# A fused FFT filter and ELU feed-forward kernel: the first eleven steps regrouped in small PSUM tiles, the last step issued one step earlier

## The chip, the core and the metric

The kernel runs on one core of a Trainium2 chip. The metric is the device time of one execution in microseconds (us), lower is better. Beside it stands one profiled execution, taken by the hardware profiler, from which all durations here come.

The engines: PE (TensorE, matmuls), ACT (ScalarE), DVE (VectorE), POOL (GpSimd), SP (issues DMAs), and the DMA queues. Each engine takes its instructions in the order in which the program hands them over, and waits on semaphores of others.

## The reference: what is computed

For 8 batches of a sequence of 3008 rows by 256 columns:

```python
X = np.fft.rfft(x, axis=1)
Yr = Xr @ w_r - Xi @ w_i + b_r
Yi = Xr @ w_i + Xi @ w_r + b_i
Y = soft_threshold(Yr, 0.01) + 1j * soft_threshold(Yi, 0.01)
y = np.fft.irfft(Y, n=3008, axis=1).astype(np.float32)
h = y.reshape(8 * 3008, 256) @ moe_w_in          # 256 -> 2048
g = np.where(h > 0, h, np.exp(np.minimum(h, 0)) - 1)
out = g @ moe_w_out                              # 2048 -> 256
```

So: a Fourier transform over the sequence, a complex matrix product with bias, a soft threshold, the transform back, and a two-layer feed-forward net with an ELU between its layers.

## The kernel before, in words

**The Fourier part.** 3008 is taken as 47 times 64, and each transform is two small matrix products with a trip through DRAM between them. Per batch there are units named by their kind: A (6 of them: M1 times x, `unit_A`, matmuls at line 145), X (8: `unit_X`, line 176), M (12: the complex product, `unit_M`, line 193), B (6: `unit_B`, line 245) and Y (8: `unit_Y`, line 400, which write `yT`, the transposed input of the feed-forward net). A is stored to DRAM (`DA`), and `load_Z` brings it back in the order that X wants; B is stored to `DB`, and `load_Bs` brings it back for Y. Each unit writes one PSUM tile of two banks and copies it out, mostly on ACT (`evac`, lines 126 and 128).

**The feed-forward part.** Tokens go in blocks of 512, hidden columns in pairs of 128. One step is one pair of one block: 8 steps to a block, 47 steps to a batch (`PER`), 376 steps in all (`n`). A step's first layer, `front`, is four matmuls into the tile `hps` (line 844, halves s = 0 and 1, each a bank of 512 columns). Then the ELU: Exp on ACT from `hps` to `Et`, a clamp of `Et`, and a combination with `hps` on DVE into `gT`. There are three ways: for a step with no unit beside it, and for step 0, in halves, Exp at line 853, clamp on POOL at line 881, combination at line 869; for a step with an M unit, two ACT passes (lines 855 and 856) and line 869; otherwise Exp on the whole tile (line 858), clamp on DVE (line 883), combination at line 871. The second layer, `back`, is eight matmuls (line 902) that add into two one-bank tiles `ps_o` over the block's eight steps; after the eighth, the block is copied to `osb` (line 913) and stored (line 920).

**The order of the work is written out by hand** in the last loop. Step i issues: the units that `plan` puts in `f0`, then `front(i)`, then the `gT` of step i-1 (`finish_elu`), then what `plan` puts in `f1`, then the clamp of step i (`elu`), then `back(i-2)`. A Fourier unit so rides along with nearly every step, and works on the next batch.

**PSUM** has eight banks: `psF`, one tile of two banks, used by all units in turn and by `front` in every third of some free steps; `psH`, two tiles of two banks for `front`; `psO`, two banks for `back`. Before the loop, batch 0 is brought through the Fourier part alone, with pools of its own that are closed one after the other; the last of these (`lateA`, `chain`, `lateB`) hold `turn_back` (line 368), `first_Y` (line 386), half of an A unit of batch 1 (`spare_A`, line 290) and the third B unit of batch 0 (`split_B`, line 309).

**The first eleven steps** work on batch 0 while the rest of its Y units and the A units of batch 1 are still to be done. `plan(0)` puts the A units u = 1 to 5 of batch 1 in `f1` of steps 0 to 4, and the Y units u = 2 to 7 of batch 0 in `f0` of steps 5 to 10. `load_Bs` for those Y units is in `f1` of steps 1 and 3, `load_Z` for batch 1 in `f1` of step 5; a scaling of a quarter of `w_in` (line 707, DVE) is in `f1` of steps 1 to 4. The X units of batch 1 begin at step 11.

**The last step** is 375: after its `front` come `back(373)`, `back(374)` and `back(375)`; its clamp runs half on DVE and half on POOL, halves are hidden columns, and the second layer takes all of half 0 first.

Of the kernel before, what the change touches and what calls it, by code (L numbers as in the profile page):

```python
# [19 lines left out]
N1 = 47  # L20
# [9 lines left out]
def kernel(  # L30
# [96 lines left out]
        else:  # L127
            nc.scalar.copy(dst, src)  # L128

    def unit_A(b, u, alone=False, on_dve=False, ahead=False):  # L130
# [12 lines left out]
        ps = unit_ps("aps", alone or ahead)  # L143
        for j in range(2):
            nc.tensor.matmul(  # L145
                ps[:, j, :], lhsT=M1[:],
                rhs=xt[:, 4 * uu + 2 * j : 4 * uu + 2 * j + 2, :], start=True, stop=True,
            )
        evac(
            A[:, 4 * uu : 4 * uu + 4, :].rearrange("p n d -> p (n d)"),  # L150
            ps[:].rearrange("p a b -> p (a b)"), on_dve,
        )
# [210 lines left out]
    def turn_back(dt):  # L363

        for h in range(2):
            ps = one_bank()
            for j in range(4):
                nc.tensor.matmul(
                    ps[0 : 16 * NT, j * P : j * P + P],
                    lhsT=turned[0][:, dt, 4 * h + j, :], rhs=idm[:], start=True, stop=True,  # L370
                )
            evac(
                Bs_of[0, 0][0 : 16 * NT, 4 * h : 4 * h + 4, dt * P : dt * P + P],
                ps[0 : 16 * NT, :].rearrange("p (m d) -> p m d", d=P), bool(h),
            )

    def first_Y(dt):

        if dt == 0:
            yT_of[0] = late2.tile([P, 2, S], BF16, name="yT", tag="yT")  # L380
        yv = yT_of[0][:, dt, 0:WT].rearrange("p (r j) -> p r j", j=8)
        for h in range(2):
            ps = one_bank()
            pv = ps[:].rearrange("p (k j) -> p k j", j=P)[:, :, 0 : 2 * N1]
            for j in range(4):
                nc.tensor.matmul(
                    pv[:, j], lhsT=Bs_of[0, 0][:, 4 * h + j, dt * P : dt * P + P], rhs=M4[:],
                    start=True, stop=True,
                )
            evac(yv[:, :, 4 * h : 4 * h + 4], pv.rearrange("p j r -> p r j"), bool(h))  # L390
# [390 lines left out]
    for h, w in enumerate((w40, w41)):  # L781
# [3 lines left out]
    gate(Bs_of[0, 0][64:96, 0, 0:1])  # L785
    load_w_out(1)
    first.close()
    lateA, chain, lateB = (
        second.enter_context(
            tc.tile_pool(name=n_, bufs=k_, space=bass.MemoryType.PSUM, reuse_waits="tile")  # L790
        )
        for n_, k_ in (("lateA", 2), ("chain", 4), ("lateB", 2))
    )
    turn_back(0)
    turn_back(1)
    keep_A = spare_A()
    first_Y(0)
    first_Y(1)
    keep_B = split_B(2, two_banks(lateB, "lateB"), True)
    keep_A()  # L800
    keep_B()
    scale_w_in(1, True, 1)
    second.close()

    psF = ctx.enter_context(
        tc.tile_pool(name="psF", bufs=1, space=bass.MemoryType.PSUM, reuse_waits="tile")
    )
# [3 lines left out]
    psO = ctx.enter_context(  # L811
        tc.tile_pool(name="psO", bufs=2, space=bass.MemoryType.PSUM, reuse_waits="tile")
    )


    g_of = {}
# [12 lines left out]
    def front(i, third, on_act, halves):  # L829
        blk, fp = divmod(i, NPAIR)  # L830
        if third:
            hps = psF.tile([P, 2, TB], F32, name="hps", tag="fps")
        else:
            hps = psH.tile([P, 2, TB], F32, name="hps", tag="hps")
        todo = []
        for s in range(2):
            ft = 2 * fp + s
            for piece in sorted(pieces(blk * TB, TB), key=lambda z: z[3] - z[2]):
                todo.append((s, ft, piece))
        if i == PER // NPAIR * NPAIR:  # L840
            todo.sort(key=lambda z: z[2][0])
        for s, ft, (b, t0, c0, c1) in todo:
            for dt in range(2):
                nc.tensor.matmul(  # L844
                    hps[:, s, c0:c1], lhsT=w_in_s[:, dt, ft * P : ft * P + P],
                    rhs=yT_of[b][:, dt, t0 : t0 + c1 - c0],
                    start=(dt == 0), stop=(dt == 1),
                )
        Et = late3.tile([P, 2, TB], F32, name="Et", tag="Et")
        E_ = Et[:]  # L850
        if halves:
            for s in range(2):
                nc.scalar.activation(E_[:, s], hps[:, s], AF.Exp)  # L853
# [7 lines left out]
    late_elu = []  # L861

    def finish_elu():
        for i, hps, Et, whole, halves in late_elu:
            gT = late3.tile([P, 2, TB], F32R, name="gT", tag="gT")
            for s in range(2) if halves else (slice(0, 2),):
                o, h, e = gT[:, s], hps[:, s], Et[:, s]
                if whole:
                    nc.vector.scalar_tensor_tensor(o, e, -1.0, h, ALU.add, ALU.max)  # L869
                else:  # L870
                    nc.vector.scalar_tensor_tensor(o, h, 0.0, e, ALU.max, ALU.add)  # L871
            g_of[i] = gT
        late_elu.clear()

    def elu(i, hps, Et, on_pool, on_act):

        E_ = Et[:]
        if on_pool:
            for s in range(2):
                eng = nc.vector if i == n - 1 and s == 0 else nc.gpsimd  # L880
                eng.tensor_scalar(E_[:, s], E_[:, s], 1.0, 0.0, ALU.min, ALU.max)  # L881
        elif not on_act:
            nc.vector.tensor_scalar(E_, E_, 1.0, -1.0, ALU.min, ALU.add)  # L883
        late_elu.append((i, hps, Et, on_pool or on_act, on_pool))

    def back(i, split):
# [7 lines left out]
            ]  # L894
        po = po_of[blk]
        order = [(q, s) for q in range(nq) for s in range(2)]
        if i == n - 1:
# [12 lines left out]
        last = i == n - 1  # L910
        for q in range(nq):
            copy = nc.vector.tensor_copy if (last and q) or (split and q == 0) else nc.scalar.copy
            copy(osb[:, 2 * q : 2 * q + 2, :], po[q][:])  # L913
            for i_ in range(2 * q, 2 * q + 2):
                for b, t, c0, c1 in pieces(bs + i_ * P, P):
                    ov = out[b * S : b * S + S, :].rearrange("(r w j) e -> w r j e", w=4, j=8)
                    while c0 < c1:
                        w, r0 = t // WT, t % WT // 8
                        k = min(c1 - c0, (w + 1) * WT - t)
                        (nc.scalar if last and i_ % 2 == 0 else nc.sync).dma_start(  # L920
                            ov[w, r0 : r0 + k // 8], osb[c0 : c0 + k, i_, :]
                        )
                        t, c0 = t + k, c0 + k
# [5 lines left out]
    def plan(b):  # L929
# [10 lines left out]
        if n1 < B:  # L940
# [4 lines left out]
                xs = (3, 8, 13)  # L945
                seq += [("A", 5), ("n", 0), ("n", 1)]
            else:
                seq = (
                    [("a", u) for u in range(1, 6)] + [("y", u) for u in range(2, 8)]
                    + [u for u in mid if u[0] != "A"]  # L950
                    + [("A", 0), ("A", 1), ("n", 0), ("n", 1)]
                    + [("A", u) for u in range(2, 6)]
                )
                xs = (10, 13, 16)
        else:
            lead, seq = 0, [("y", u) for u in range(2, 8)]
        for t, u in enumerate(seq, lead):
            if u[0] == "y":
                f0[t].append(put("Y", b, u[1]))
            elif u[0] == "n":  # L960
                f0[t].append(put("Y", n1, u[1]))
            elif u[0] == "a":
                f1[t].append(put("A", n1, u[1]))
            elif u[0] == "A":
                if n2 < B:
                    f0[t].append(put("A", n2, u[1]))
# [8 lines left out]
        if b == 0:  # L975
            for t in range(4):
                f1[t + 1].append((scale_w_in, (2 + t // 2, True, t % 2)))
            f1[1].append((load_Bs, (0, 1)))
            f1[3] += [(load_Bs, (0, w)) for w in (2, 3)]
            f1[5] += [(load_Z, (1, s0, s1)) for s0, s1 in ((0, 8), (8, NS))]  # L980
# [5 lines left out]

    f0 = f1 = None
    bare = 0
    for i in range(n + LAG):
        if i < n:  # L990
            r = i % PER
            if r == 0:
                f0, f1 = plan(i // PER)
# [7 lines left out]
            h = front(i, calm and bare % 3 == 1, on_act, free or i == 0)  # L1001
        finish_elu()
        if i < n:
            for f, a in f1[r]:
# [1 line left out]
            split = i > LAG and (i - LAG) % NPAIR == NPAIR - 1  # L1006
            if split:
                back(i - LAG, True)
            elu(i, *h, free or i == 0, on_act)
        else:  # L1010
            split = False
        if i >= LAG and not split:
            back(i - LAG, False)


# [28 lines left out]
```

## Time and profile before

| what | value |
|---|---|
| times of the runs shown | 908.20, 910.53, 910.32 us; median 910.32 |
| the profiled execution's own time | 908.42 us |
| its span | 906.6 us |
| granted TensorE clock, mean | 0.999 |
| busy: PE / DVE / ACT / POOL | 888.8 / 719.7 / 698.5 / 312.8 us |
| HBM traffic | 116 GB/s over the span |

The span is what the profile covers, from first to last recorded work; the execution's own time is 1.8 us more. "Busy" sums the durations of an engine's instructions. The profile has these views: a timeline of instructions (start, duration, engine, line, operation, output and inputs, count), a list of waits, a table of busy time in stretches, a chain of work that ended last, and groups of instructions by line.

### The profile page before, as it was taken

What the parts mean: (1) busy time and instruction counts of PE and PEld (TensorE: products, weight loads), DVE (VectorE), ACT (ScalarE), POOL (GpSimd) and SP (SyncE); (2) the same over time, 40 slices, a digit from 0 to 9 for tenths busy, and PEclk for the clock granted to TensorE, in tenths of its full rate; (3) what the DMA queues carried; (4) which work ended last, traced back from release to release, by engine and by line L of the source; (5) the groups of instructions that cost most, each with busy time, mean ns of one, the idle gap of its engine ahead of it and who ended that gap; (6) DMA issues with size and microseconds to landing.
All of it is one profiled execution on the core that took longest, in us unless ns stands there. A gap on an engine that the chain in (4) does not pass through costs nothing.

```text
span 906.6 us, 17374 instructions
## 1 busy us (share of the span) xinstructions
PE 888.8 (98%) x6767; PEld 652.3 (72%) x6767; DVE 719.7 (79%) x899; ACT 698.5 (77%) x857; POOL 312.8 (34%) x436
## 2 busy tenths in 40 slices
PE   8889999999999999999999999999999999999997
PEld 3458667776678676876678766787667867777776
DVE  8779778887788778887788877888778877778776
ACT  6688778787878788788787888778887877777664
POOL 6710440133331431405404153133332134443664
PEclk9999999999999999999999999999999999999999
DMA  8988025821383215723176032752228111231011
GB/s 263 315 242 252 25 71 158 238 70 48 94 231 117 71 48 156 197 91 93 52 204 186 26 105 59 212 161 77 65 75 228 31 42 47 82 83 48 24 47 47
DMA packets 90655, 106.06 MB, mean 117 GB/s; under 512 B 5302, under 2 KB 81340, under 8 KB 87212
## 3 DMA queue, kind: packets, MB, share of 16 engines
q1 hardware_dynamic: 84316, 77.42, 30.9%
q0 software_dynamic: 5968, 27.26, 9.1%
q8 instruction: 53, 0.87, 0.4%
q10 hardware_dynamic: 288, 0.26, 0.1%
q14 instruction: 30, 0.25, 0.1%
HBM read 55.12 MB, written 49.81 MB: 116 GB/s over the span
## 4 chain that ended last, share of the span: by engine, by line
PE 85%; DMA 4%; DVE 4%; ACT 3%; issue 2%; POOL 1%; SPq 0%; DVEq 0%; ACTq 0%; POOLq 0%
PE ps_o L902 34%; PE hps L844 34%; PE mps L193 9%; PE yps L400 2%; PE bps L245 2%; PE aps L145 2%; PE xps L176 2%; DMA DB<-Bz 1%; DMA Z<-DA 1%; DVE gT L871 1%; DMA xt<-in_x_dram 1%; DMA Bs<-DB 1%; DVE Et L883 1%; DVE gT L869 1%; ACT Et L858 1%
## 5 line engine op out<-in xcount | busy, mean ns | idle before, releaser
L902 PE MATMUL ps_o<-w_out_r,gT 128*128 128x256 f32 x3008 | 476.6, 301 | 0.2 <-DVE gT L869 0.2
L902 PEld LDWEIGHTS ps_o<-w_out_r,gT 128*128 128x128 f32 x3008 | 403.5, 189 | 49.9 <-DVE osb L913 1.3
L844 PE MATMUL hps<-yT,w_in_s 128*128 128x512 bf16 (+4 forms) x1728 | 388.7, 352 | 1.3 <-DVE gT L871 0.3
L869 DVE SCALAR_TENSOR_TENSOR gT<-Et,hps 128x512 fp32r<-128x512 f32 (+1 forms) x268 | 220.3, 851 | 74.3 <-POOL Et L881 38.2
L871 DVE SCALAR_TENSOR_TENSOR gT<-hps,Et 128x1024 fp32r<-128x1024 f32 x200 | 244.7, 1223 | 15.8
L844 PEld LDWEIGHTS <-w_in_s 128*128 128x128 bf16 x1728 | 141.7, 98 | 128.7 <-issue 20.7
L858 ACT ACTIVATE Et<-hps 128x1024 f32<-128x1024 f32 x200 | 206.1, 1030 | 10.2 <-PE hps L844 3.5
L881 POOL TENSOR_SCALAR Et<-Et 128x512 f32<-128x512 f32 x183 | 109.1, 615 | 221.7 <-ACT Et L853 218.7
L883 DVE TENSOR_SCALAR Et<-Et 128x1024 f32<-128x1024 f32 x200 | 138.4, 692 | 47.9 <-ACT Et L858 40.2
L211 POOL TENSOR_SCALAR clip<-yb 128x512 f32<-128x512 f32 x84 | 51.6, 615 | 317.1 <-DVE yb L203 279.6
L853 ACT ACTIVATE Et<-hps 128x512 f32<-128x512 f32 x184 | 99.9, 595 | 63.7 <-PE hps L844 63.7
L855 ACT ACTIVATE Et<-hps 128x1024 f32<-128x1024 f32 x84 | 86.3, 1027 | 71.9 <-PE hps L844 71.4
L212 POOL TENSOR_TENSOR Y<-yb,clip 128x512 bf16<-128x512 f32 x84 | 107.2, 1277 | 7.0
L856 ACT ACTIVATE Et<-Et 128x1024 f32<-128x1024 f32 x84 | 88.8, 1057 | 2.7
L203 DVE TENSOR_TENSOR yb<-mps,bias_bc 128x512 f32<-128x512 f32 x89 | 61.3, 689 | 35.4 <-PE mps L193 26.8
L128 ACT CAST XT<-xps 128x768 bf16<-128x768 f32 x61 | 48.7, 800 | 17.1 <-PE xps L176 17.1
L193 PE MATMUL mps<-wcat_r,XT 128*128 128x512 bf16 x192 | 58.2, 384 | 1.0 <-ACT Bz L258 0.5
L128 ACT CAST yT<-yps 128x752 bf16<-128x752 f32 x62 | 48.9, 789 | 12.5 <-PE yps L400 12.4
L193 PE MATMUL mps<-wcat_s,XT 128*128 128x512 bf16 x192 | 57.1, 379 | 0.0
L128 ACT CAST A<-aps 128x1024 bf16<-128x1024 f32 x45 | 45.6, 1014 | 13.8 <-PE aps L145 12.0
L193 PEld LDWEIGHTS <-XT 128*128 128x128 bf16 x384 | 30.9, 98 | 29.8 <-issue 0.7
L258 ACT CAST Bz<-bps 128x1024 bf16<-128x1024 f32 x45 | 45.0, 1001 | 2.1 <-PE bps L245 2.1
(132 smaller groups left out, 415.4 us busy)
## 6 DMA issues: line engine op xcount, KB each, us to landing
xt<-in_x_dram POOLq DMA_DIRECT2D x21, 1024.0 KB, 7.3
out_dram<-osb SPq DMA_DIRECT2D x158, 128.0 KB
Bs<-DB SPq DMA_DIRECT2D x30, 384.0 KB
DA<-A SPq DMA_DIRECT2D x20, 512.0 KB
DB<-Bz SPq DMA_DIRECT2D x20, 512.0 KB
Z<-DA SPq DMA_DIRECT2D x7, 1152.0 KB
Z<-DA SPq DMA_DIRECT2D x11, 384.0 KB
xt<-in_x_dram POOLq DMA_DIRECT2D x6, 512.0 KB, 6.2
```

The lines of the kernel that those rows point to most:

```text
L128: nc.scalar.copy(dst, src)
L193: nc.tensor.matmul(ps, lhsT=XT[:, dt, c, o : o + P], rhs=wm[:, dt, :], start=(not biased and m == 0 and dt == 0), stop=(m == 1 and dt == 1),)
L212: nc.gpsimd.tensor_tensor(Y_of[b, q][:, i, :], yb, clip[:], ALU.subtract)
L844: nc.tensor.matmul(hps[:, s, c0:c1], lhsT=w_in_s[:, dt, ft * P : ft * P + P], rhs=yT_of[b][:, dt, t0 : t0 + c1 - c0], start=(dt == 0), sto ...
L853: nc.scalar.activation(E_[:, s], hps[:, s], AF.Exp)
L856: nc.scalar.activation(E_, E_, AF.Exp, scale=-1.0)
L858: nc.scalar.activation(E_, hps[:], AF.Exp)
L869: nc.vector.scalar_tensor_tensor(o, e, -1.0, h, ALU.add, ALU.max)
L871: nc.vector.scalar_tensor_tensor(o, h, 0.0, e, ALU.max, ALU.add)
L881: eng.tensor_scalar(E_[:, s], E_[:, s], 1.0, 0.0, ALU.min, ALU.max)
L883: nc.vector.tensor_scalar(E_, E_, 1.0, -1.0, ALU.min, ALU.add)
L902: nc.tensor.matmul(po[q][:, i_ % 2, :], lhsT=gT[:, s, i_ * P : i_ * P + P], rhs=w_out_r[:, ft, :], start=(ft == 0 and i_ % 2 == 0), stop=( ...
```

## The change

1. **No `psF` in the first eleven steps** (`FILL = 11`). Its two banks are two one-bank tiles of a pool `psG` until step 11. The A and Y units of these steps use one `psG` tile for each half, and each half has its own copy out (half 0 on ACT, half 1 on DVE; both on ACT for the A unit of step 1). `split_Y` is the new form of a Y unit.
2. **Units moved**: A units to steps 1, 3, 4, 5, 6; Y units to steps 7 to 10, two in steps 7 and 10; `load_Bs` to steps 2, 4, 5; `load_Z` to step 6; the next x loads on POOL from steps 10, 13, 16 to 12, 15, 18.
3. **ELU of steps 0 to 10** always in halves with the clamp on POOL, and the Exp of half 0 is handed over between the two halves of the first layer (`early`).
4. **`back(0)` goes ahead of `front(2)`**, and takes all of half 0 first.
5. **The last step**: `front(375)` is issued ahead of `back(372)`, in `psF`; its Exp, clamp and combination are split by tokens instead of hidden columns, the clamp all on POOL; its second layer is in the usual order; the second half of the last block is copied out and stored in two pieces. In the last batch the steps that use `psF` are shifted by one.
6. **Before the loop**: `turn_back` and `first_Y` swap ACT and DVE for their two copies; the copy of `split_B` goes half to ACT; the late pools change their places.

```diff
+        if apart:
+            pair = two_banks(psG, "gps")
+            banks = [t[:] for t in pair]
...
-                ps[0 : 16 * NT, :].rearrange("p (m d) -> p m d", d=P), bool(h),
+                ps[0 : 16 * NT, :].rearrange("p (m d) -> p m d", d=P), not h,
...
+    def split_Y(b, u):
+        w, dt = u // 2, u % 2
+        yv = yT_of[b][:, dt, w * WT : w * WT + WT].rearrange("p (r j) -> p r j", j=8)
+        for h, t in enumerate(two_banks(psG, "gps")):
+            pv = t[:].rearrange("p (k j) -> p k j", j=P)[:, :, 0 : 2 * N1]
+            for j in range(4):
+                nc.tensor.matmul(
+                    pv[:, j], lhsT=Bs_of[b, w][:, 4 * h + j, dt * P : dt * P + P], rhs=M4[:],
+                    start=True, stop=True,
+                )
+            evac(yv[:, :, 4 * h : 4 * h + 4], pv.rearrange("p j r -> p r j"), bool(h))
...
-    keep_B = split_B(2, two_banks(lateB, "lateB"), True)
+    keep_B = split_B(2, two_banks(lateB, "lateB"), False)
...
+        early = i < FILL
         for s, ft, (b, t0, c0, c1) in todo:
             for dt in range(2):
                 nc.tensor.matmul(
                     hps[:, s, c0:c1], lhsT=w_in_s[:, dt, ft * P : ft * P + P],
...
+            if early and (dt, c1) == (1, TB):
+                nc.scalar.activation(E_[:, s], hps[:, s], AF.Exp)
+        if early:
+            return hps, Et
+        if i == n - 1:
+            for h in range(2):
+                t = slice(TB // 2 * h, TB // 2 * h + TB // 2)
+                nc.scalar.activation(E_[:, :, t], hps[:, :, t], AF.Exp)
...
+            for t, u in ((1, 1), (3, 2), (4, 3), (5, 4), (6, 5)):
+                f1[t].append((unit_A, (1, u, False, t > 1, True)))
+            for t, a, u in ((7, f0, 2), (7, f1, 3), (8, f0, 4), (9, f0, 5), (10, f0, 6), (10, f1, 7)):
+                a[t].append((split_Y, (0, u)))
+            for t, w in ((2, 1), (4, 2), (5, 3)):
+                f1[t].append((load_Bs, (0, w)))
...
+        if i == LAG:
+            back(0, False)
...
-            elu(i, *h, free or i == 0, on_act)
+            elu(i, *h, free or i < FILL, on_act)
+            if i == n - 2:
+                early_h = front(n - 1, True, False, True)
```

More of the change, by code (lines that the diff above doesn't have):

```diff
@@ L128, in evac, with unit_A @@
             nc.scalar.copy(dst, src)
-    def unit_A(b, u, alone=False, on_dve=False, ahead=False):
+    def unit_A(b, u, alone=False, on_dve=False, apart=False):
         ci, uu = u // 2, u % 2
@@ L142, in unit_A @@
         dav = DA_of[b].rearrange("j p d -> p j d")
-        ps = unit_ps("aps", alone or ahead)
+        if apart:
+            pair = two_banks(psG, "gps")
+            banks = [t[:] for t in pair]
+        else:
+            ps = unit_ps("aps", alone)
+            banks = [ps[:, j, :] for j in range(2)]
         for j in range(2):
             nc.tensor.matmul(
-                ps[:, j, :], lhsT=M1[:],
+                banks[j], lhsT=M1[:],
                 rhs=xt[:, 4 * uu + 2 * j : 4 * uu + 2 * j + 2, :], start=True, stop=True,
             )
[L149 to L152, printed above, removed]
+        Af = A[:, 4 * uu : 4 * uu + 4, :].rearrange("p n d -> p (n d)")
+        if apart:
+            for j in range(2):
+                evac(Af[:, 512 * j : 512 * j + 512], banks[j], on_dve and bool(j))
+        else:
+            evac(Af, ps[:].rearrange("p a b -> p (a b)"), on_dve)
         j0 = 8 * ci
@@ L387, in first_Y @@
                     pv[:, j], lhsT=Bs_of[0, 0][:, 4 * h + j, dt * P : dt * P + P], rhs=M4[:],
+                    start=True, stop=True,
+                )
+            evac(yv[:, :, 4 * h : 4 * h + 4], pv.rearrange("p j r -> p r j"), not h)
+    def split_Y(b, u):
[6 more added lines that the diff above has]
+                    pv[:, j], lhsT=Bs_of[b, w][:, 4 * h + j, dt * P : dt * P + P], rhs=M4[:],
                     start=True, stop=True,
@@ L787 @@
     first.close()
-    lateA, chain, lateB = (
+    chain, lateB, lateA = (
         second.enter_context(
@@ L791 @@
         )
-        for n_, k_ in (("lateA", 2), ("chain", 4), ("lateB", 2))
+        for n_, k_ in (("chain", 4), ("lateB", 2), ("lateA", 2))
     )
@@ L803 @@
     second.close()
-    psF = ctx.enter_context(
-        tc.tile_pool(name="psF", bufs=1, space=bass.MemoryType.PSUM, reuse_waits="tile")
-    )
     psH = ctx.enter_context(
@@ L813 @@
     )
+    few = ExitStack()
+    psG = few.enter_context(
+        tc.tile_pool(name="psG", bufs=2, space=bass.MemoryType.PSUM, reuse_waits="tile")
+    )
+    FILL = 11
     g_of = {}
@@ L841, in front @@
             todo.sort(key=lambda z: z[2][0])
+        Et = late3.tile([P, 2, TB], F32, name="Et", tag="Et")
+        E_ = Et[:]
+        early = i < FILL
         for s, ft, (b, t0, c0, c1) in todo:
@@ L848, in front @@
                 )
-        Et = late3.tile([P, 2, TB], F32, name="Et", tag="Et")
-        E_ = Et[:]
-        if halves:
+            if early and (dt, c1) == (1, TB):
[6 more added lines that the diff above has]
+                nc.scalar.activation(E_[:, :, t], hps[:, :, t], AF.Exp)
+        elif halves:
             for s in range(2):
@@ L861, with parts @@
     late_elu = []
+    np_all = (slice(0, P), slice(0, 2), slice(0, TB))
+    def parts(i):
+        if i == n - 1:
+            return [
+                (slice(0, P), slice(0, 2), slice(h, h + TB // 2)) for h in (0, TB // 2)
+            ]
+        return [(slice(0, P), s, slice(0, TB)) for s in range(2)]
     def finish_elu():
@@ L865, in finish_elu @@
             gT = late3.tile([P, 2, TB], F32R, name="gT", tag="gT")
-            for s in range(2) if halves else (slice(0, 2),):
-                o, h, e = gT[:, s], hps[:, s], Et[:, s]
+            for s in parts(i) if halves else (np_all,):
+                o, h, e = gT[s], hps[s], Et[s]
                 if whole:
@@ L878, in elu @@
         if on_pool:
-            for s in range(2):
-                eng = nc.vector if i == n - 1 and s == 0 else nc.gpsimd
-                eng.tensor_scalar(E_[:, s], E_[:, s], 1.0, 0.0, ALU.min, ALU.max)
+            for s in parts(i):
+                nc.gpsimd.tensor_scalar(E_[s], E_[s], 1.0, 0.0, ALU.min, ALU.max)
         elif not on_act:
@@ L896, in back @@
         order = [(q, s) for q in range(nq) for s in range(2)]
-        if i == n - 1:
+        if i == 0:
             order = [(q, s) for s in range(2) for q in range(nq)]
@@ L912, in back @@
             copy = nc.vector.tensor_copy if (last and q) or (split and q == 0) else nc.scalar.copy
-            copy(osb[:, 2 * q : 2 * q + 2, :], po[q][:])
+            if not (last and q):
+                copy(osb[:, 2 * q : 2 * q + 2, :], po[q][:])
             for i_ in range(2 * q, 2 * q + 2):
+                if last and q:
+                    copy(osb[:, i_, :], po[q][:, i_ % 2, :])
                 for b, t, c0, c1 in pieces(bs + i_ * P, P):
@@ L919, in back @@
                         k = min(c1 - c0, (w + 1) * WT - t)
-                        (nc.scalar if last and i_ % 2 == 0 else nc.sync).dma_start(
+                        (nc.scalar if last and i_ % 2 else nc.sync).dma_start(
                             ov[w, r0 : r0 + k // 8], osb[c0 : c0 + k, i_, :]
@@ L947, in plan @@
             else:
-                seq = (
-                    [("a", u) for u in range(1, 6)] + [("y", u) for u in range(2, 8)]
-                    + [u for u in mid if u[0] != "A"]
+                lead, seq = 11, (
+                    [u for u in mid if u[0] != "A"]
                     + [("A", 0), ("A", 1), ("n", 0), ("n", 1)]
@@ L953, in plan @@
                 )
-                xs = (10, 13, 16)
+                xs = (12, 15, 18)
         else:
@@ L961, in plan @@
                 f0[t].append(put("Y", n1, u[1]))
-            elif u[0] == "a":
-                f1[t].append(put("A", n1, u[1]))
             elif u[0] == "A":
@@ L977, in plan @@
                 f1[t + 1].append((scale_w_in, (2 + t // 2, True, t % 2)))
-            f1[1].append((load_Bs, (0, 1)))
-            f1[3] += [(load_Bs, (0, w)) for w in (2, 3)]
-            f1[5] += [(load_Z, (1, s0, s1)) for s0, s1 in ((0, 8), (8, NS))]
+            for t, u in ((1, 1), (3, 2), (4, 3), (5, 4), (6, 5)):
[4 more added lines that the diff above has]
+                f1[t].append((load_Bs, (0, w)))
+            f1[6] += [(load_Z, (1, s0, s1)) for s0, s1 in ((0, 8), (8, NS))]
             f1[xs[0]].append((lambda: gate(Z_of[1][:, 16, 0:1]), ()))
@@ L988 @@
     bare = 0
+    early_h = None
     for i in range(n + LAG):
-        if i < n:
+        if i == FILL:
+            few.close()
+            psF = ctx.enter_context(
+                tc.tile_pool(name="psF", bufs=1, space=bass.MemoryType.PSUM, reuse_waits="tile")
+            )
+        if i == LAG:
+            back(0, False)
+        if early_h:
+            h, on_act = early_h, False
+        elif i < n:
             r = i % PER
@@ L1000 @@
             on_act = any(f is unit_M for f, a in f0[r])
-            h = front(i, calm and bare % 3 == 1, on_act, free or i == 0)
+            h = front(i, calm and bare % 3 == (2 if i // PER == B - 1 else 1), on_act, free or i < FILL)
         finish_elu()
@@ L1008 @@
                 back(i - LAG, True)
-            elu(i, *h, free or i == 0, on_act)
+            elu(i, *h, free or i < FILL, on_act)
+            if i == n - 2:
+                early_h = front(n - 1, True, False, True)
+            elif early_h:
+                early_h = None
         else:
             split = False
-        if i >= LAG and not split:
+        if i > LAG and not split:
             back(i - LAG, False)
```

## The prediction, made before the changed kernel was run

> **What bounds the kernel now.** I read the busy times first, then busy times in stretches, then the waits and the timeline of the two stretches that the change touches.
>
> ```profile
> PE 888.8 (98%) x6767; PEld 652.3 (72%) x6767; DVE 719.7 (79%) x899; ACT 698.5 (77%) x857; POOL 312.8 (34%) x436
> ```
>
> PE is busy 98% of the span. Between 158 and 850 us, stretches of about 100 us hold 95.3 to 99.9 us of PE work: nothing is to be had there, and what is lost or won early reaches the end. The changed program is the same from step 11 up to the last steps, but for which of batch 7's free steps use `psF`, and PE is full there too. So two places count: steps 0 to 10 (51.9 to 77.4 us) and the tail (895 to 907 us). Of the first, four stretches of 2 us:
>
> ```profile
> 54.00:56.00 2.00, 1.21 (x5) 0.49 (x4) 1.51 (x3) 2.00 (x4) 1.04 (x2) 1.00 1.15 314
> 62.00:64.00 2.00, 1.11 (x9) 0.89 (x7) 1.90 (x4) 1.68 (x2) 0.00 (x0) 1.00 0.86 245
> 64.00:66.00 2.00, 1.50 (x15) 1.11 (x16) 0.84 (x1) 0.87 (x2) 0.00 (x0) 1.00 1.14 367
> 66.00:68.00 2.00, 2.00 (x22) 1.57 (x20) 0.92 (x2) 1.72 (x2) 0.00 (x0) 1.00 1.00 259
> ```
>
> The first column after the length is PE. It idles around 55 and 63 us and is full from 66. The waits of 51.9 to 77.4 name the causes:
>
> ```profile
> PEld L400 <- DMA Bs<-DB: 1.6, 1, 1.6
> PEld aps L145 <- ACT A L128: 1.4, 2, 1.2
> ...
> PE yps L400 <- DMA Bs<-DB: 1.4, 1, 1.4
> ```
>
> The first Y unit waits for `Bs` from DRAM, and A units queue for the single `psF` tile until ACT has emptied it. How large is the hole? The timeline has the first front at 51.92, the first Y at 64.50, the first X at 77.43. The six Y steps take 12.93, 2.155 each, without a wait. In the tail a step of only front and back takes 1.80 (fronts at 895.45 and 897.25), so a front (four matmuls) is about 0.86 and a back 0.94; a Y is 0.35; an A, taken from the 2.28 of the step from 58.39 to 60.67, is 0.47. Steps 0 to 4 up to the first Y hold 5 fronts, 5 A and 3 backs: 4.3 + 2.35 + 2.8 = 9.45. They take 12.58. **The hole is 3.1 us**; the change can win no more there.
>
> **Part 1, a wait that the change puts in.** In the changed program as built, `front` of steps 0 to 10 stands on PE thus (here step 3):
>
> ```
> Matmult hps<-yT,w_in_s 128x512 [waits DVE]
> Matmult hps<-yT,w_in_s 128x512
> Matmult hps<-yT,w_in_s 128x512 [waits Activation]
> Matmult hps<-yT,w_in_s 128x512
> ```
>
> The third matmul is the first of half 1. The count that it waits for is reached by the Exp of half 0 of this same tile; I followed it for all eleven steps. The two halves are different banks, yet PE stops until ACT has read half 0. The kernel before has no such wait: there both Exps come after all four matmuls. PE runs in order, so behind this matmul stand the rest of the front, the A or Y unit of `f1` and the back: nothing covers it. Its price comes from these rows:
>
> ```profile
> 51.92 1.04 PE L844 MATMUL hps<-yT,w_in_s 128*128 128x512 bf16 x4 [0.22 <-DVE yT L126]
> ...
> 52.99 1.09 ACT L853 ACTIVATE Et<-hps 128x512 f32<-128x512 f32 x2 [0.97 <-PE hps L844]
> ```
>
> Four matmuls started at 51.92 release ACT at 52.99, 1.07 later; two are 0.43 shorter, 0.64. An Exp of a half lasts 0.596 (the 184 of line 853). From ACT to PE it takes 0.05 (the copy begun at 53.96 lasts 1.02, the A matmul it releases starts at 55.03). So half 1 starts 0.64 + 0.60 + 0.05 = 1.29 after half 0 instead of 0.43: **0.86 per front, 9.4 over eleven**. No trace shows this round trip itself; from below I bound a front's loss by the 0.73 that PE lost to one copy on ACT at 55.03 (8.0 in all), from above by 0.95, if ACT comes 0.1 late (10.5).
>
> **Part 2, what the regrouping gives back.** I lay the steps out by hand with these durations. A front takes 1.72, a step with A 1.72 + 0.47 + 0.94 = 3.13, with one Y 3.0, with two 3.36. Beside that ACT needs two Exps and one copy (1.2 + 0.6), DVE 1.29 for `gT`, 0.68 for its half of a copy and in steps 1 to 4 0.42 for the scaling, together 2.4; POOL 1.2 for the clamps. All fit, so PE alone paces the steps.
>
> - Swapped copies before the loop: `turn_back`'s two on ACT last 1.06, on DVE 1.28, and DVE starts first now; `first_Y` likewise. Gain 0.2: front(0) near 51.75.
> - Step 0: ACT now copies half of `lateB` (0.6), to 52.9, where Exp was ready at 52.4: loss 0.5. Step 1: its first Exp stands behind step 0's second: 0.2.
> - `back(0)` ahead of `front(2)`: `front(2)` needed `gT` of step 0 anyway, and finds it done at 56.3. No cost.
> - Y units from step 7, at about 71: `Bs`, there at 64.4 before, no longer stops PE. Units in two banks are copied out by two engines at once. With these the old hole of 3.1 is gone, but into time that PE now loses in Part 1.
> - `load_Z`: step 6's A copies end near 71, so `DA` is stored 7 us later than before (63.70 on SP's queue), `Z` asked for at some 75 to 76 (a 256 KB store took 2.8 at 15.75; 4.5 for 512 KB, an estimate). `Z` was complete 9.6 after its request (70.19 to POOL's gate at 79.8), so at 85; its first part, a quarter, by 79. X begins at 84.0 and wants the rest at 88.6. Hidden with 3 to spare; POOL's gate and the x loads behind it come 6 us later, and the M units that queue behind them start 8 steps after the X.
>
> Sum: 9.4 + 0.5 + 0.2 - 0.2 - 3.1 = **+6.8**; between 8.0 - 3.1 - 1.0 = +4 (if ACT's delays of steps 0 and 1 don't arise and more is gained) and 10.5 + 0.7 - 2.5 = +8.7.
>
> **Part 3, the tail.**
>
> ```profile
> 897.25 1.04 PE L844 MATMUL hps<-yT,w_in_s 128*128 128x512 bf16 x4
> ...
> 899.61 1.29 DVE L869 SCALAR_TENSOR_TENSOR gT<-Et,hps 128x512 fp32r<-128x512 f32 x2
> 900.35 1.34 PE L902 MATMUL ps_o<-w_out_r,gT 128*128 128x256 f32 x8 [0.19 <-DVE gT L869]
> 901.53 0.59 ACT L913 COPY osb<-ps_o 128x512 f32<-128x512 f32 x1 [2.12 <-issue]
> 901.73 0.69 DVE L913 COPY osb<-ps_o 128x512 f32<-128x512 f32 x1 [0.83 <-PE ps_o L902]
> 902.15 1.48 ACTq L920 DMA_DIRECT2D out_dram<-osb  x2
> ```
>
> `front(375)` moves to 896.31. Its Exps follow step 374's on ACT at 897.6, the clamps follow on POOL at 898.4 to 899.6, `gT` runs 899.1 to 900.4. Three backs fill PE from 897.2 to 900.0; `back(375)` starts then on the first tokens and ends at 900.96, against 901.5 before. The copies in pieces put the last store on its queue at 902.1 instead of 902.9 (the second of the two in the last line). The 3 us from there to the span's end stay. Gain **0.8**; 0.3 if the pieces give nothing, 1.1 at best.
>
> Whole: +6.8 - 0.8 = +6.0 on the profiled execution's 908.42 gives 914.4; on the median of the runs shown, 910.32, it gives 916.3. I take **915.3**, between them.
>
> **Rivals.**
>
> *A: the wait costs nothing, faster than before.* If PE goes on to half 1 without waiting out the Exp (below 0.25 per front the loss falls under the hole), the layout without it reaches X at about 75.6, 1.8 earlier (3.1 less about 0.5 while `gT` of step 0 is awaited, 0.4 while that of step 1 is, and 0.4 at the tight copies of the first Y units), with the tail 2.6: 906.7. For it: the halves are in different banks, and nothing in the arithmetic asks for the wait. Against it: the wait stands in the program, and PE does stop at such waits (the 0.7 for `aps` above). The Trainium skill, PSUM — Partial Sum Buffer, section on bank collisions, says that only accesses to the same bank and quadrant collide and that different banks run clean; by that rule the wait isn't needed, and rival A would be the time. This program waits all the same, so I give it 0.06.
>
> *B: less is lost.* The round trip overlaps more than I see, or waits that I add fall together: 0.6 per front, 6.6 - 3.1 - 0.8 = +2.7, 912 on the middle of the runs. For it: modelled ends of matmuls are drawn long. Against it: the 1.07 is from start to start of two engines. 0.10.
>
> *C: PE's clock drops.* PE will idle some 0.9 in every 3.1 us for 32 us. Before, 62 to 64 us had 1.11 busy of 2.00 and the granted clock stayed 1.00; 54 to 56 likewise; it fell to 0.66 only at 905 to 907, after 3 us without a matmul. If it fell to half for half of the stretch, its 22 us of matmuls (11 fronts, 9 backs, 6 Y, 5 A) would cost 11 more: 926. The Trainium skill, TensorE: Matmul & The Clock Gate, section on psum-queue depth-cycling, tells of a kernel whose frequent short PE idles between matmul groups made the clock oscillate. The rows here speak against it: 0.03.
>
> *D: a late transfer on top.* `Z` or the last quarter of `w_in` lands later than laid out and adds 1 to 3: 917 to 918. `Z` has 3 us to spare: 0.04.
>
> **Chances.** Forecast 0.77, A 0.06, B 0.10, C 0.03, D 0.04. A difference of 0.3% (2.7 us) is about what a measurement of this kernel can tell from none. Faster by more: A, part of it at the edge, 0.05. Slower by more, above 913.05: all of C and D, and nine tenths of the forecast, 0.77. The rest, 0.18, lies within. The range runs from 911.6 (908.42 + 4.0 - 0.8; B's middle, 912, lies in it) to 918.7 (910.32 + 8.7 - 0.3).
>
> **What would show it.** Right, if fronts of steps 0 to 10 stand in the timeline as two pairs some 1.3 us apart, PE's waits name ACT `Et` for about 9 us in eleven places, the first X unit begins near 84 us, and the last matmul stands 5 to 6 us later than before. The hole at the first Y should be gone, and the tail from front(375)'s place to the end 0.8 shorter. Wrong, if the four matmuls of a front follow each other, if X begins before 78, or if the granted clock falls under 1.00 between 52 and 84 us.

## The result, and the profile after

| | kernel before | changed kernel |
|---|---|---|
| median of 6 runs | 909.67 us (908.20 to 910.53) | **915.79 us** (914.84 to 916.24) |
| ratio to before, 95% interval | | **1.0068** (1.0055 to 1.0081): slower by 6.1 us |
| profiled execution: time, span | 908.42, 906.6 | 915.80, 914.0 |
| granted TensorE clock, mean | 0.999 | 0.999 |

The forecast was 915.3. The page of the changed kernel has the busy times, and a new wait in the groups of instructions (columns: what and how many; busy time and mean ns of one; idle time of the engine just before them, and what ended most of it):

```profile
PE 884.7 (97%) x6664; PEld 652.4 (71%) x6767; DVE 718.9 (79%) x908; ACT 696.5 (76%) x869; POOL 325.3 (36%) x457
```

```profile
L869 PE MATMUL hps<-yT,w_in_s 128*128 128x512 bf16 (+7 forms) x1650 | 383.3, 351 | 13.3 <-ACT Et L875 7.9
```

PE is at 97% now (6664 matmul records stand beside 6767 weight loads, so some 100 records are missing and the busy time is a little low). It stands idle ahead of the first layer's matmuls for 7.9 us because of ACT's `Et`, that is the Exp. The list of PE's waits says how often, from the first front to the first X unit (us in total, times, longest). It has one entry:

```profile
PE hps L869 <- ACT Et L875: 7.9, 11, 0.9
```

Eleven waits for eleven fronts. The busy times in stretches of 4 us (length, then busy time of PE, PEld, DVE, ACT, POOL; the granted clock is third from the end) show no hole any more, but a loss spread over every stretch:

```profile
54.00:58.00 4.00, 3.27 (x18) 2.06 (x17) 2.67 (x6) 2.60 (x5) 1.76 (x3) 1.00 1.33 348
58.00:62.00 4.00, 2.62 (x15) 1.87 (x15) 3.74 (x7) 2.32 (x5) 1.94 (x4) 1.00 0.68 190
62.00:66.00 4.00, 3.32 (x19) 2.46 (x19) 1.93 (x4) 2.08 (x4) 1.74 (x3) 1.00 0.31 101
66.00:70.00 4.00, 3.31 (x25) 2.60 (x24) 2.58 (x4) 2.34 (x5) 1.81 (x3) 1.00 0.83 227
```

Before, 66 to 68 us was full; here PE lacks 0.7 of 4 us even there. No other engine is full throughout either (DVE comes nearest, with 3.74 of 4 in the second stretch): PE waits for ACT, and ACT is busy for little more than half the time. The timeline of step 4 (start, duration; in brackets idle time before and what ended it) shows the round trip itself:

```profile
60.54 0.60 PE L869 MATMUL hps<-yT,w_in_s 128*128 128x512 bf16 x2
...
61.18 0.60 ACT L875 ACTIVATE Et<-hps 128x512 f32<-128x512 f32 x1 [0.78 <-PE hps L869]
...
61.83 0.59 PE L869 MATMUL hps<-yT,w_in_s 128*128 128x512 bf16 x2 [0.68 <-ACT Et L875]
```

Half 0 starts at 60.54, ACT 0.64 later, half 1 at 61.83: 0.64 + 0.60 + 0.05 = 1.29 after half 0, in place of the 0.43 that two matmuls take from start to start. The list's 7.9 is less than eleven times 0.86 because it counts only from the end drawn for half 0's matmuls, 0.60 after their start. By the starts of the halves the eleven waits add up to 9.8: half 1 starts 1.48 after half 0 in the first front and 1.28 to 1.37 in the other ten (where one row holds the matmuls of two fronts, half 0 is put 0.43 after the row's start; one record that is missing, in front(8), is filled in). The next front starts at 63.67, so the step takes 3.13. In the tail the timeline answers to the one of before:

```profile
903.65 1.90 PE L869 MATMUL hps<-yT,w_in_s 128*128 128x512 bf16 x8
905.20 4.13 PE L941 MATMUL ps_o<-w_out_r,gT 128*128 128x256 f32 x32
...
908.93 0.59 ACT L953 COPY osb<-ps_o 128x512 f32<-128x512 f32 x1 [2.14 <-issue]
909.37 0.76 DVE L956 COPY osb<-ps_o 128x256 f32<-128x256 f32 x2 [0.83 <-PE ps_o L941]
909.55 1.49 ACTq L962 DMA_DIRECT2D out_dram<-osb  x2
```

The two last fronts stand together, the backs behind them run as one row of 32 matmuls, and the last copy is in pieces. From front(374) to the end of the span it is 10.35 instead of 11.15.

**Where the 7.4 us between the two spans went**, from the starts of `turn_back`, front(0), the first X unit and front(374) in both timelines:

| stretch | before | changed | difference |
|---|---|---|---|
| up to `turn_back` | 48.75 | 47.55 | -1.20 |
| `turn_back` to front(0) | 3.17 | 3.00 | -0.17 |
| front(0) to first X unit | 25.51 | 32.25 | **+6.74** |
| first X unit to front(374) | 818.02 | 820.85 | +2.83 |
| front(374) to the end | 11.15 | 10.35 | -0.80 |

The first row is no work of the change: the program is the same up to there, and `turn_back` starts anywhere from 47.24 to 48.75 in the twelve profiles of this document, at 47.40 in a second one of the kernel before. The fourth is nearly all waits of two Y units for `Bs` in batches 1 and 7, which the section on the experiments comes back to. What remains is 6.74 - 0.17 - 0.80 = +5.8; the medians differ by 6.1.

### The profile page after: what moved, and what is told of

The parts are those of the page before. It is cut to its first block, busy times and chain, and to the rows that moved or that the text cites. A ratio compares the mean times of both kernels' runs of the same rounds, so it can differ in the third digit from the quotient of the medians.

```text
span 914.0 us, 17319 instructions
## 1 busy us (share of the span) xinstructions
PE 884.7 (97%) x6664; PEld 652.4 (71%) x6767; DVE 718.9 (79%) x908; ACT 696.5 (76%) x869; POOL 325.3 (36%) x457
## 4 chain that ended last, share of the span: by engine, by line
PE 85%; ACT 5%; DVE 4%; issue 3%; DMA 2%; POOL 1%; SPq 0%; DVEq 0%; ACTq 0%; POOLq 0%
PE ps_o L941 34%; PE hps L869 33%; PE mps L200 9%; PE yps L420 2%; PE bps L252 2%; PE xps L183 2%; PE aps L150 2%; DVE gT L911 1%; DMA Bs<-DB 1%; ACT Et L886 1%; ACT Et L889 1%; DVE Et L922 1%; ACT Bz L265 1%; DMA DB<-Bz 1%; ACT Et L875 1%
## 5 line engine op out<-in xcount | busy, mean ns | idle before, releaser
L869 PE MATMUL hps<-yT,w_in_s 128*128 128x512 bf16 (+7 forms) x1650 | 383.3, 351 | 13.3 <-ACT Et L875 7.9
L909 DVE SCALAR_TENSOR_TENSOR gT<-Et,hps 128x512 fp32r<-128x512 f32 (+1 forms) x288 | 233.1, 839 | 76.4 <-POOL Et L920 37.8
L911 DVE SCALAR_TENSOR_TENSOR gT<-hps,Et 128x1024 fp32r<-128x1024 f32 x190 | 232.4, 1223 | 14.8
L920 POOL TENSOR_SCALAR Et<-Et 128x512 f32<-128x512 f32 x204 | 121.7, 613 | 240.2 <-ACT Et L884 220.4
L889 ACT ACTIVATE Et<-hps 128x1024 f32<-128x1024 f32 x190 | 195.8, 1030 | 8.7 <-PE hps L869 2.3
L922 DVE TENSOR_SCALAR Et<-Et 128x1024 f32<-128x1024 f32 x190 | 131.5, 692 | 49.1 <-ACT Et L889 41.6
L884 ACT ACTIVATE Et<-hps 128x512 f32<-128x512 f32 x180 | 97.7, 595 | 62.3 <-PE hps L869 60.8
L886 ACT ACTIVATE Et<-hps 128x1024 f32<-128x1024 f32 x84 | 86.2, 1026 | 72.1 <-PE hps L869 70.5
L200 PE MATMUL mps<-wcat_r,XT 128*128 128x512 bf16 x180 | 55.6, 385 | 1.0 <-ACT Bz L265 0.5
L128 ACT CAST yT<-yps 128x752 bf16<-128x752 f32 x56 | 44.1, 788 | 12.5 <-PE yps L420 12.4
L128 ACT CAST A<-aps 128x1024 bf16<-128x1024 f32 x42 | 42.5, 1014 | 13.2 <-PE aps L150 11.5
```

The costliest lines, as they stand in the source:

```text
L200: nc.tensor.matmul(ps, lhsT=XT[:, dt, c, o : o + P], rhs=wm[:, dt, :], start=(not biased and m == 0 and dt == 0), stop=(m == 1 and dt == 1),)
L869: nc.tensor.matmul(hps[:, s, c0:c1], lhsT=w_in_s[:, dt, ft * P : ft * P + P], rhs=yT_of[b][:, dt, t0 : t0 + c1 - c0], start=(dt == 0), sto ...
L920: nc.gpsimd.tensor_scalar(E_[s], E_[s], 1.0, 0.0, ALU.min, ALU.max)
```

## The experiments

**Theory**: the wait of half 1 for the Exp of half 0 costs all of the loss, and what the regrouping wins is lost inside it. **Rival**: the new layout (two engines for a unit's copies, units moved, late `Z`) is slow by itself. The runs' stretches, waits for `Bs` of the first Y unit of batch 1 and of batch 7, and times:

| kernel | front(0) to X | front(374) to end | waits for `Bs` | median | ratio to before (95%) |
|---|---|---|---|---|---|
| before | 25.51 | 11.15 | 0 / 0.55 | 909.67 | |
| before, again (e6) | 25.84 | 11.31 | 1.66 / 0.43 | 909.09, one run | |
| changed | 32.25 | 10.35 | 1.41 / 1.61 | 915.79 | 1.0068 (1.0055 to 1.0081) |
| changed, again (e8) | 32.18 | 10.33 | 1.96 / 0.50 | 915.50, one run | |
| e1: Exp after all four matmuls | 25.55 | 10.43 | 0.66 / 1.25 | 908.46 | 0.9996 (0.9985 to 1.0007) |
| e2: `hps` as two tiles | 25.53 | 10.31 | 1.66 / 1.48 | 910.00 | 1.0008 (0.9999 to 1.0017) |
| e3: wait in 8 more fronts | 32.15 | 10.31 | 1.51 / 0.36 | 923.69 | 1.0172 (1.0153 to 1.0191) |
| e4: before, with the wait | 34.69 | 11.21 | 0.91 / 0.88 | 918.45 | 1.0105 (1.0092 to 1.0119) |
| e5: e2 in other banks | 24.73 | 10.41 | 1.57 / 1.34 | 908.20 | 0.9989 (0.9977 to 1.0001) |
| e7: before, with parts 5 and 6 | 27.71 | 10.39 | 1.13 / 0.90 | 909.64 | 1.0005 (0.9994 to 1.0017) |
| e9: e5, A units earlier | 24.36 | 10.34 | 1.77 / 0.91 | 907.76 | 0.9984 (0.9975 to 0.9993) |
| e10: e9, Y of batch 7 later | 24.22 | 10.35 | 1.27 / 0 | 906.22 | 0.9965 (0.9952 to 0.9979) |

The kernel before, run beside them on the same chips, had medians of 909.13 (e1 to e4), 908.97 (e5 to e8) and 909.10 (e9, e10).

**e1: both Exps after all four matmuls.**

```diff
-        early = i < FILL
+        early = False
```

> The changed kernel with one thing undone: both Exps of a step come after all four matmuls of its first layer, in all steps; everything else of the change stays. Theory (the wait of half 1 on the Exp of half 0 costs 0.86 us in each of eleven fronts): PE's waits on ACT Et vanish, front(0) to the first X unit takes 24.5 us (24 to 25.5) instead of 32.25, time 908.0 (906.5 to 909.5). Rival (the moved units, the small PSUM tiles or the clamps on POOL cost the time): 31 to 33 us still, time 914 to 916.

The loss is gone: 908.46, no difference from before that the interval shows. PE's waits from 50.8 to 76.5 us no longer name the Exp:

```profile
PE ps_o L941 <- DVE gT L909: 0.8, 1, 0.8
PE gps L406 <- ACT A L128: 0.3, 1, 0.3
PE hps L869 <- DVE gT L909: 0.3, 1, 0.3
PE xps L183 <- ACT yT L128: 0.2, 1, 0.2
PE gps L406 <- ACT yT L128: 0.2, 1, 0.2
```

So handing over the Exp early costs 32.25 - 25.55 = **6.70 us**, and the rival falls as the cause of the loss. But my own expectation of 24.5 was too good too: with the Exp back in its place the regrouped start takes 25.55, as long as the old one with its hole (25.51 and 25.84).

**e2 and e5: the interleaved Exp kept, the tile cut in two.** The rule that the prediction weighed for rival A was that halves in different banks don't need the wait. In steps 0 to 10 `hps` becomes two tiles of one bank each, so that the Exp of half 0 and the matmuls of half 1 touch different tiles (`psE` takes the banks of `psH` until step 11; `Two` picks the tile by the half; the `gT` of step 10 is now handed over ahead of the units of step 11, before the pools change):

```diff
+        elif i < FILL:
+            hps = Two([psE.tile([P, TB], F32, name="hps", tag="hpe") for _ in range(2)])
```

e5 changes only the order in which the pools are opened, and so the banks:

```diff
-    chain, lateB, lateA = (
+    lateB, chain, lateA = (
...
+    psE = few.enter_context(...)
     psG = few.enter_context(...)
-    psE = few.enter_context(...)
```

> The changed kernel with the early Exp kept, but in steps 0 to 10 the two halves of the first layer are two one-bank tiles instead of one tile of two banks. Theory (the wait comes from treating the two-bank tile as one thing, not from reading one bank while another is written): the wait is gone, front(0) to the first X unit 23.8 us (23 to 25), time 907.3 (906 to 909), as Exp can start 0.43 us earlier than in e1_exp_after_front. Rival (reading one bank on ScalarE while PE writes the next slows PE, or the early Exp hurts in another way): above 26 us and 911 or more.

> e2_two_tiles with its pools laid on other banks, so that front(0) no longer waits for the copy of lateB (0.98 us lost there) and the first X unit no longer for gT of step 10 (1.39 lost). Theory: turn_back to front(0) 3.0 us again instead of 3.98, front(0) to the first X unit 24.1 instead of 25.53, so 1.4 us less there than in e1_exp_after_front; time 907.0 (905.5 to 908.5). Rival (reading a bank while the next is written has a price, and the two losses only cover it): front(0) to the first X unit stays at 25.5.

e2 misses its expectation: 25.53 and 910.00, where 23.8 and 907.3 were expected. The waits for the Exp are gone, but two others came. PE's waits of 47 to 78 us begin:

```profile
PE xps L183 <- DVE gT L920: 1.4, 1, 1.4
PE hps L880 <- ACT Bz L128: 1.0, 1, 1.0
```

The first is the first X unit, which takes a bank that the ELU of step 10 still reads; the second is front(0), in a bank that the last copy before the loop still reads. Both follow from where the pools lie. In e5 they are gone, and 24.73 and 908.20 come near the 24.1 and 907.0 expected. The timeline of its first fronts shows what the changed kernel might have done:

```profile
54.94 1.90 PE L880 MATMUL hps<-yT,w_in_s 128*128 128x512 bf16 x8
...
55.58 2.06 ACT L886 ACTIVATE Et<-hps 128x512 f32<-128x512 f32 x4 [0.93 <-PE hps L880]
```

ACT reads half 0 0.64 after PE's start, as before, while PE goes on with half 1 and the next front, eight matmuls without a stop. The wait belonged to the two-bank tile and not to the chip. The Trainium skill, PSUM — Partial Sum Buffer, section "PSUM bank collisions raise a hardware error", says that accesses to different banks run clean; e5 agrees, with 0 us waited where the changed kernel waited 7.9. With the interleaving free, e5 is 0.8 ahead of e1 in the stretch (24.73); measured against e5, which keeps the early Exp, the wait itself costs 32.25 - 24.73 = 7.52. e5 then meets a late transfer: its first three X units start at 75.39, 77.69 and 81.31, the third with this wait:

```profile
77.69 0.52 PE L183 MATMUL xps<-M,Z 96*128 96x96 bf16 x8
81.31 0.51 PE L183 MATMUL xps<-M,Z 96*128 96x96 bf16 x8 [1.31 <-DMA Z<-DA]
```

That is rival D's place; the wait in the changed kernel had hidden it by making everything ahead of it late.

**e3: the wait in eight more fronts.** Steps 11 to 18 too hand over the Exp between the halves; with that goes their ELU in halves and with the clamp on POOL, as in steps 0 to 10 (not in the lines shown).

```diff
+    EARLY = 19
...
-        early = i < FILL
+        early = i < EARLY
```

> The changed kernel with the early Exp, in halves with the clamp on POOL, in steps 0 to 18 instead of 0 to 10: eight more fronts get the wait, beside X units. Theory: a step with an X unit takes 3.0 us instead of 2.15, 8 x 0.86 = 6.9 us more, time 922.7 (921 to 924). Rival (the loss belongs to the start, where latency and DMA rule): no more than 1 us on top, 915 to 917.

Measured 923.69, where 922.7 was expected. From the first X unit to front(19) the profiled runs take 27.12 (82.39 to 109.51) against 18.04 in the changed kernel (82.80 to 100.84): 9.08 for eight, or **1.13 each** where 0.86 was expected. The list of PE's waits has nineteen for the Exp now, 16.1 in all. The sign and the place are the theory's; the size is not, and the timeline tells why:

```profile
85.99 0.60 PE L870 MATMUL hps<-yT,w_in_s 128*128 128x512 bf16 x2
86.19 0.80 ACT L128 CAST XT<-xps 128x768 bf16<-128x768 f32 x1 [0.67 <-PE xps L183]
...
86.89 0.60 ACT L876 ACTIVATE Et<-hps 128x512 f32<-128x512 f32 x1
...
87.54 0.59 PE L870 MATMUL hps<-yT,w_in_s 128*128 128x512 bf16 x2 [0.95 <-ACT Et L876]
```

Half 0 starts at 85.99, so ACT could begin at 86.63. But the X unit's copy, all of it on ACT, came first, and the Exp starts at 86.89. The wait takes in whatever ACT has in front of the Exp. In the changed kernel a unit's copy is shared with DVE and mostly out of the way.

**e4: the wait in the kernel before.** Its first eleven steps get the Exp between the halves; its hole at the first Y unit stays.

```diff
+        early = i < 11
...
+            if early and (dt, c1) == (1, TB):
+                nc.scalar.activation(E_[:, s], hps[:, s], AF.Exp)
+        if early:
+            return hps, Et
```

> The kernel before with one part of the change alone: in steps 0 to 10 the Exp of half 0 is handed over between the two halves of the first layer; the clamp stays where it was, the units too. Theory: 0.86 us more in each of steps 5 to 10, which had no slack (5.2 us), and 4.3 us less most of the 3.1 us hole in steps 0 to 4 (0.5 to 2.5 net); front(0) to the first X unit 32.0 us (31 to 33.5) instead of 25.5, time 916.2 (914.5 to 918). Rival (the wait costs only together with the regrouped units): 25.5 to 26.5 us, 909 to 911.

Measured 918.45; front(0) to the first X unit takes 34.69, 9.2 more than before, where I had expected the hole to take up more. The list of PE's waits of 51 to 86 us has the eleven in full:

```profile
PE hps L847 <- ACT Et L853: 10.7, 11, 1.2
```

What they displace is only the 1.4 for `Bs` and the 0.7 for the copy of A in the list of before: 10.7 - 2.1 = 8.6 of the 9.2. And they are dearer than in the changed kernel, since the copy of a whole unit tile on ACT stands ahead of the Exp, as the timeline shows:

```profile
56.36 1.01 ACT L128 CAST Bz<-aps 128x1024 bf16<-128x1024 f32 x1
57.25 0.61 ACT L853 ACTIVATE Et<-hps 128x512 f32<-128x512 f32 x1
...
57.91 0.59 PE L847 MATMUL hps<-yT,w_in_s 128*128 128x512 bf16 x2 [1.18 <-ACT Et L853]
```

Where that copy is out of the way, the wait is 0.7 here too (at 61.09 and 64.19). So the regrouping is worth something, but only where the wait is: 32.25 against 34.69 with it, 25.55 against 25.51 without.

**e7: the kernel before with only the tail and the swapped copies (parts 5 and 6).** Its edit is those parts of the change's diff and nothing else; of part 6, the late pools stay where they were. With it ran both kernels unmodified (e6, e8), to see how the stretches vary by themselves.

> The kernel before with parts 5 and 6 of the change alone (the last step ahead and by tokens; the swapped copies before the loop), steps 0 to 10 as before. Theory: front(374) to the end 10.35 us instead of 11.15, turn_back to front(0) 3.0 instead of 3.17, no wait of half 1; time 908.2 (907 to 909.5), a ratio of about 0.999. Rival (the tail gains only beside the other parts): 11.15 and no difference.

> The kernel before, unchanged, for a second profile: how much its waits of the first Y units of batches 1 and 7 for Bs vary (0 and 0.55 us in the first profile, 1.41 and 1.61 in the changed kernel). If these waits vary by themselves, 0.5 to 3 us together; if the change makes them, 0.6 or less again. Time 908 to 911.

> The changed kernel, unchanged, for a second profile: front(0) to the first X unit 32.2 us again (it hangs on fixed durations); the two waits for Bs together anything from 0.5 to 3.2 us if they vary by themselves, about 3 if the change makes them. Time 914.5 to 916.5.

The two gains are there alone (`turn_back` to front(0) 3.00, tail 10.39), and yet the time is 909.64 against 908.97 beside it, unchanged within the interval and a miss: 908.2 and a ratio of 0.999 were expected. In the profiled run the start ate them: 27.71 in place of 25.51 and 25.84. PE's timeline and the busy times in stretches of 1 us:

```profile
64.00 0.51 PE L400 MATMUL yps<-M,Bs 96*128 96x94 bf16 x8 [2.02 <-DMA Bs<-DB]
...
67.31 0.85 PE L400 MATMUL yps<-M,Bs 96*128 96x94 bf16 x8
```

```profile
63.00:64.00 1.00, 0.00 (x1) 0.01 (x1) 0.70 (x1) 0.00 (x0) 0.00 (x0) 1.00 1.11 341
64.00:65.00 1.00, 0.94 (x10) 0.66 (x12) 0.00 (x0) 0.46 (x1) 0.00 (x0) 0.90 1.22 390
65.00:66.00 1.00, 1.00 (x4) 0.74 (x3) 0.00 (x0) 0.49 (x2) 0.00 (x0) 0.50 1.03 243
...
68.00:69.00 1.00, 1.00 (x8) 0.55 (x6) 0.92 (x1) 0.79 (x1) 0.00 (x0) 0.90 0.70 213
```

The swapped copies bring front(0) 0.17 earlier, and `Bs` no sooner: PE waits 2.02 for it, where the kernel before waited 1.40 and 1.75. The rest of the difference, 0.1 to 0.5, is when `Bs` lands. Then the granted clock falls to 0.50 from about 64.8 to 68.2, and the two Y steps in it take 3.31 and 2.59 in place of 2.15: some 1.6 lost.

This explains the profiled run and not the median. Some 3.4 us at half the clock take about 0.002 off the mean clock of a run, and the mean is on record for every run. The profiled run has 0.997; three of the twelve runs of e7 have 0.997 or 0.998, and they are its three slowest (910.91, 911.44, 912.50). The other nine have 0.999 or 1.000, and the median lies among them. Nor is the drop e7's own: 12 of the 23 runs of the kernel before beside it have 0.998 or less. Where in the span the clock fell in those isn't on record.

**e9 and e10: e5 mended.** e9 puts the A units in steps 1 to 5 without the empty step 2, and `load_Z` and the last `load_Bs` one step earlier. e10 also issues the first two Y units of batch 7 three steps later, where a free step is.

```diff
-            for t, u in ((1, 1), (3, 2), (4, 3), (5, 4), (6, 5)):
+            for t, u in ((1, 1), (2, 2), (3, 3), (4, 4), (5, 5)):
...
-            for t, w in ((2, 1), (4, 2), (5, 3)):
+            for t, w in ((2, 1), (4, 2), (4, 3)):
...
-            f1[6] += [(load_Z, (1, s0, s1)) for s0, s1 in ((0, 8), (8, NS))]
+            f1[5] += [(load_Z, (1, s0, s1)) for s0, s1 in ((0, 8), (8, NS))]
```

```diff
-                seq += [("A", 5), ("n", 0), ("n", 1)]
+                seq += [("A", 5)] + [("-",)] * (3 * (n2 == B)) + [("n", 0), ("n", 1)]
```

> e5_two_tiles_banks with the A units in steps 1 to 5 instead of 1, 3, 4, 5, 6 and load_Z in step 5 instead of 6. Theory: e5's X units waited 1.31 us for Z because its last A unit stands a step later than in the kernel before; with it a step earlier Z is asked for some 2 us earlier and the wait is gone; front(0) to the third X unit 28.9 us instead of 30.65; time 907.0 (905.5 to 908.5), ratio to the kernel before 0.9975. Rival (DMA traffic, not the A unit, sets when Z lands): the wait stays above 1 us.

> e9_a_units_earlier with the first two Y units of batch 7 three steps later (steps 41 and 42 of batch 6). Theory: their wait for Bs, 0.36 to 1.61 us in the profiles so far, goes, since 5.4 to 6.5 us more lie between the load and its use; time 0.9 less than e9's, 906.1 (904.5 to 908). Rival (the wait moves to the next use of Bs, or the steps lose what the units gave them as cover): no difference.

In e9 the third X unit waits for nothing (X units at 77.23 and 79.38, the usual 2.15 apart), and the median of 907.76 lies within the range expected. In e10 the Y unit of batch 7 no longer waits either; the list of PE's waits for `Bs` from 100 to 903 us has one left:

```profile
PE yps L420 <- DMA Bs<-DB: 1.3, 1, 1.3
```

e10 is faster than both kernels: 906.22, ratio to before 0.9965 (0.9952 to 0.9979), where the changed kernel has 1.0068. Its median is 1.5 below e9's, more than the 0.9 expected. This last step would suit the kernel before too, which waited 0.55 and 0.43 at that Y unit; that wasn't run. By the start alone, e9 is at 0.9984 (0.9975 to 0.9993).

**What stays open.** The waits of batches 1 and 7 for `Bs` add up to 0.55 and 2.09 in two executions of the kernel before, 1.79 and 2.03 with its start in e4 and e7, and 1.87 to 3.14 in the kernels with the regrouped start (e10 aside). They vary from one execution to the next by as much as they would have to differ, so whether the regrouping makes them longer, by about 1 us, isn't settled. Nor is it known why the gains of e7's two parts, about 1 us together in its profile, don't show in its median.

## Why the prediction was right

The time (915.79 for 915.3) and the mechanism were right: the third matmul of each front waits for ACT, and this makes the kernel slower. By its steps:

- **Part 1, the wait: right in size.** Start to start 1.29 was worked out from rows that showed no such round trip. 1.28 to 1.37 was measured in ten fronts and 1.48 in the first. With 0.7 for ACT's copies ahead of the first two Exps, 10.1 was laid out; 9.8 was measured: the first two fronts exceed 1.29 by 0.24 together and not by 0.7. PE's list of waits has 7.9, where "about 9" was given as the sign.
- **The steps laid out with the wait were right**, and this is what the kernel does: 3.13 for a step with A (60.54 to 63.67), 3.0 for one Y (76.31 to 79.32, 3.01), 3.36 for two (79.32 to 82.80, 3.48). From front(0) to X the prediction has 84.0 - 51.75 = 32.25, and 32.25 was measured. That it fits to the last digit is luck: the working's own durations add up to 32.5.
- **Part 2, what the regrouping gives back: the term that was mis-sized.** Without any stall the working's durations add up to 22.4 from front(0) to X (two steps with a front alone, five with an A, two with one Y, two with two). For a layout without the wait the prediction priced 1.3 of stalls (rival A) and had X 23.85 after front(0) (51.75 to 75.6), 1.7 less than in the kernel before. e5, which is that layout, has 2.3 of stalls and takes 24.73, 0.8 less. e1, with the Exp late, has 3.2 and takes no less at all. By the starts in e1's timeline these are 1.3 around the first back, 0.6 at the fronts behind it, 0.4 ahead of the first Y unit, and 0.4 and 0.5 in the two steps with two Y units. The five waits of e1's list, 1.8, are only what lies behind the drawn ends of matmuls.
- **Why the sum came out all the same.** In the changed kernel the eleven waits, 9.8, and the 22.4 make up the whole 32.25: the other stalls pass while PE waits for the Exp anyway. So the sum of durations was right, and what each term would bring by itself was not. Taking the early Exp away brings 6.70 and not 9.4, since some 3 of stalls come up in its place; the regrouping, put at 0.7 - 3.1 = -2.4 in the sum, brings +0.04 without it. The two errors cancel because both terms leave out the same stalls.
- **`Z` and the swapped copies.** `DA` was stored at 69.97 (71 laid out), `Z` asked for at 73.35 (75 to 76), and X started at 82.80 without a wait: hidden, as said. All of it came 1.0 to 2.6 earlier than laid out, 1.2 of that because front(0) was at 50.55. e5 shows how close it was: with steps a little faster, `Z` is late by 1.31. The gain of 0.2 ahead of front(0) measured 0.17.
- **Part 3, the tail**: 0.8 predicted, 0.80 measured, and 0.76 to 0.92 in e7 against the two profiles of before. The sign that the last matmul would stand 5 to 6 later missed: it ends 7.6 later (909.33 for 901.69), 2.8 of it from the stretch between X and front(374).
- **Rivals.** A fell for this program. Made real by two tiles it takes 908.20 (e5, where `Z` is late) and with that mended 907.76 (e9); 906.7 was its forecast. e10's 906.22 holds a gain in batch 7 that the rival didn't have. B fell: the waits don't overlap (9.8 by the starts, where B had 6.6). C fell in the changed kernel: in every stretch of 1 us from 50 to 90 the clock was 1.00. The Trainium skill, TensorE: Matmul & The Clock Gate, section "A second HAM failure mode: psum-queue depth-cycling", tells of a kernel in which short idles made the clock oscillate. Here they did not: eleven idles of 0.7 to 0.9 in 32 us left it at 1.00, and so did the nineteen of e3 (0.7 to 1.2, from 50 to 110 us). D fell here and appeared in e5.

## What to carry to other kernels

In this program a reader handed over between two writes to one tile made the second write wait, even though the two touch different banks: PE paid 0.86 us a time, and 1.13 where another copy stood ahead of that reader. Give each part a tile of its own before the reader is moved up, and look on each engine for the wait the program holds, not for the one the arithmetic needs. And a term that is right as a duration is not what its removal brings: work out both layouts, with it and without it, or test them apart, since here each of two terms brought about 2 us less, taken by itself, than it stands for, and their sum was right.

## What the hardware showed that I had not expected

In e7 an idle of 2.02 us on PE was followed by some 3.4 us at a granted clock of 0.50. Idles of 1.40 and 1.75 at the same Y unit (the two executions of the kernel before) left it at 1.00, and so did 1.31 at an X unit (e5) and even 1.96 at a Y unit of batch 1 (e8, from 152.36 to 154.32; 1.00 in every stretch of 1 us up to 162). The Trainium skill, TensorE: Matmul & The Clock Gate, Part 1, section "What's actually happening", gives about 3.4 us for the idle window, free-running, and about as much for the way back. The way back agrees with 3.4 here; the idle ahead of it was only 2.02. One profiled run shows this, and 1.96 against 2.02 says that more than the length of the idle may decide, so it is a case and not a threshold.
